# The second half's first layer norm from a turned input, with its scales and offsets spread over the partitions through DRAM

## The chip, the cores and the metric

The kernel runs on one core of one Trainium2 chip. The metric is the device time of one execution in microseconds, and it is taken as the median of several. Of the kernel before there are three runs: 2188.53, 2188.95 and 2190.12 us, median 2188.95.

## The reference

One transformer block on 2048 rows of 1024 numbers, in float32: layer norm, an attention with a memory that is carried from one segment of 512 rows to the next, and an MLP of width 3584.

```python
def _layernorm(x, axis=-1, eps=1e-5):
    m = jnp.mean(x, axis=axis, keepdims=True)
    v = jnp.var(x, axis=axis, keepdims=True)
    return (x - m) / jnp.sqrt(v + eps)

def _A_ref(x, wq, wk, wv, wo, beta):       # H = 32 heads of 32, N = 4 segments of L = 512
    q, k, v = ...                          # x @ wq, x @ wk, x @ wv, each as B, H, N, L, 32
    for s in range(N):
        logits = einsum("bhqd,bhkd->bhqk", q[s], k[s]) * scale + mask
        a_dot = einsum("bhqk,bhkd->bhqd", softmax(logits), v[s])
        a_mem = (phi(q[s]) @ M) / (phi(q[s]) @ z + 1e-6)
        outs.append(g * a_mem + (1.0 - g) * a_dot)
        M, z = M + phi(k[s]).T @ v[s], z + phi(k[s]).sum(0)
    return outs @ wo

h = x + _A_ref(_layernorm(x), wq, wk, wv, wo, beta)
y = _layernorm(h)
out = h + gelu(y @ w1 + b1) @ w2 + b2
```

The change concerns the very first line of this for rows 1024 to 2047: `_layernorm(x)` of the second half.

## The kernel before, in words

**Halves and slices.** The 2048 rows are done in two halves of 1024, one after the other in one loop; a half has two slices (`sl`) of 512 rows, which are the segments of the attention. A half runs through these stages: layer norm 1 and attention, the product with `wo`, layer norm 2, the first MLP product ("mixer"), and in half 1 the second MLP product for both halves.

**Number format.** TensorE multiplies in a rounded format, `fp32r`. So each operand is kept as two tiles, an upper part (rounded) and a lower part (the rest), and each product is three matmuls: upper by upper, lower by upper, upper by lower. The name of a tile ends in `h` or `l` accordingly: `wh`/`wl` for weights, `yh`/`yl` for the normalised input, `zh`/`zl` for the second layer norm's. The products of q, k and v are on lines 127 to 129 (tiles `qps`, `kps`, `vps` take the results in PSUM).

**Layer norm 1.** The products want `y` turned: features on partitions, 512 rows along the free axis, as `yh`, `yl` of 128 x 8 x 512. `ln1` (L214) loads four tiles `xt` of 128 rows x 1024 features; for each, VectorE takes the statistics (L134, L138), GpSimd makes the scale r = (v + eps)^-0.5 (L141, L142) and the offset -m r (L147), and ScalarE normalises the tile in place (L182), where scale and offset are one number a partition. Then `ln_transpose` (L156) turns it: per tile two groups of four transposes of 128 x 128 on TensorE (L161) into a PSUM tile `pt`, a copy by ScalarE into `yh` (L163) and a subtraction by VectorE into `yl` (L165). A layer norm of 512 rows so has 32 transposes in 8 groups. The bank of a group is taken in turn from tags "av", "pt", "pt"; the mixer's `dps` uses tag "pt" too.

**The mixer.** The first MLP product has 28 blocks of 128 features of w1, taken as 14 pairs (block j and block j + 14) in a form of the Strassen kind: instead of eight products of half size, seven, on sums of blocks. `pair(j)` (L1139) is 20 steps of PE, in five runs of four: S1 into `dps`, S3 into `bps`, `sixth(j+1)` (S2 of the next pair, into that pair's `bps`), A22 into `bps`, S4 into `dps`. Around them:

- `fetch` loads the raw weights `r0`, `r1` (named r1 and r2 in the code) of the pair after next, and its part `p1r` of the seventh product (L1113, L1115).
- `combine` (L1117) makes their sums s1 to s4 on GpSimd (L1121 to L1124).
- `made` (L1127) splits one sum into upper and lower: a ScalarE copy (L1136) and a VectorE subtraction (L1137), into tiles `sa` (even pairs) or `sb` (odd pairs).
- `u3` (L1164) is a VectorE read of the bank `bps` after S3; the A22 product then goes on adding to that bank. `ht` (L1033) are evictions of finished sums by VectorE, followed by gelu on ScalarE.

**The end of the first half (L1500 to L1513).** Pairs 0 to 4 of the mixer run alone. Pairs 5 to 13 are interleaved with the layer norm of the second half's first slice and the first three steps of its second slice: after every PE step of the mixer 0.17 of a step of the layer norm is issued. What is left of the second slice (`acts["ahead"]`) goes on during the second half's attention, 0.55 of a step per step there (L710, L758).

```python
acts["ahead"] = ln1(1, 1, gap=2)
interleave(chain(*(mixer.pair(j) for j in range(HP - 9, HP))),
           chain(ln1(1, 0, 2), islice(acts["ahead"], 3)), 0.17)
```

**What sets the order.** Within a half `in_order()` (L107) ties every instruction of an engine to the one written before it, so each engine works in the order in which the code is written and waits in that order: an instruction that waits holds up all behind it on its engine. At the change from half 0 to half 1 this order is opened and closed again, and the instructions that stand there, outside any such block, are placed by a scheduler. Loads are issued on the queue of SyncE (SP), in order as well.

**The start of the second half.** `attention_pool` (L338) makes the tile `mask` (a memset and a select, L341, L342) and the small tile `pat` (a memset and two selects, L355 to L357) on GpSimd, and loads the memory state. `load_block` (L330) loads and splits the first weights of k and q (L103, L104: ScalarE's copy, GpSimd's subtraction `wl`). Attention then runs as 16 units of 24 steps, each a group of four heads on one slice (ORDER); in a unit come the products of k and q, then their turned and regrouped copies: `side` (L443) holds a lower part on its way by DMA into `ks` and `qs`, and `pqk` (L563) is the first product of the scores. The two buffers `ks0` and `ks1` are first filled from `pat` by a VectorE cast (L676), in the first units only. The weights of v are split in four pieces by GpSimd (L693, tiles `wl`), and `pk` (L385) is a VectorE operation on the keys.

## Time and profile before

| | us |
|---|---|
| median of three runs | 2188.95 |
| the profiled execution | 2189.65 |
| its span in the trace | 2187.9 |
| of it: first half up to mixer pair 4 | 711.76 |
| mixer pairs 5 to 13 of the first half, with layer norm 1 of the next slice | 124.69 |
| first 44.55 us of the second half, with layer norm 1 of the last slice | 44.55 |
| the rest of the second half | 1306.9 |

The view of windows gives for the same stretches the busy time of each engine (in brackets the number of instructions), the granted TensorE clock, the share of time in which the DMA engines were busy, and their rate.

```profile
0.00:711.76 711.76, 694.60 (x3778) 558.64 (x3778) 443.48 (x1067) 430.16 (x1045) 318.81 (x531) 1.00 0.52 150
711.76:836.45 124.69, 123.81 (x561) 102.18 (x560) 72.17 (x108) 52.98 (x81) 48.12 (x45) 1.00 0.56 164
836.45:881.00 44.55, 43.67 (x222) 35.02 (x220) 33.71 (x79) 26.92 (x60) 24.42 (x42) 1.00 0.59 159
881.00:2187.90 1306.90, 1297.04 (x6379) 1054.87 (x6379) 813.65 (x1443) 590.78 (x1248) 558.56 (x589) 1.00 0.59 185
```

The engines stand in the order PE, weight loads, DVE (VectorE), ACT (ScalarE), POOL (GpSimd). A row of the trace that is quoted further down begins, in the timeline, with the start of the instruction and its duration, both in us, then engine, line, operation, destination <- sources and shapes, and in brackets the idle time of the engine before it with what ended it. In the lists by line, three numbers with strokes are the shortest, middle and longest duration in ns.

### The profile page before, as it was taken

Reading aid. Unit: us, or ns where it says so; the run is one execution under the profiler, and the core shown is the slowest. Engines: PE = TensorE matmul, PEld = TensorE weight load, DVE = VectorE, ACT = ScalarE, POOL = GpSimd, SP = SyncE. Lnnn points to the kernel's source line nnn. Section 1 sums busy time; section 2 is a strip of 40 time slices with the busy share of each in tenths; the row PEclk is TensorE's granted clock in tenths of the full one; section 3 lists DMA queues with packets and bytes.
Section 4 is the critical chain, followed back from the end, with each engine's and each line's share of the span. In section 5 each row is a group of like instructions: output and inputs, shape, how many; then the busy total and the mean of one; then the engine's idle time right before and its main releaser. Section 6 shows DMA issues by size and latency. Waiting matters only on the chain.

```text
span 2187.9 us, 33209 instructions
## 1 busy us (share of the span) xinstructions
PE 2159.1 (99%) x10937; PEld 1750.7 (80%) x10937; DVE 1363.0 (62%) x2696; ACT 1100.8 (50%) x2433; POOL 949.9 (43%) x1206
## 2 busy tenths in 40 slices
PE   7999999999999999999999999999999999999999
PEld 6777777778888887877777768888887888888887
DVE  6766666665745656766667655745666765577653
ACT  5777777762543445777777652643443232323221
POOL 5533335562444434433335561534445544256330
PEclk9999999999999999999999999999999999999999
DMA  6544445664575655544444664575569775576762
GB/s 181 136 107 106 106 106 136 192 199 164 156 209 155 183 163 138 139 108 108 107 108 131 197 192 147 173 217 161 171 189 378 270 231 187 190 245 229 247 223 92
DMA packets 352405, 376.20 MB, mean 172 GB/s; under 512 B 27214, under 2 KB 244330, under 8 KB 352234
## 3 DMA queue, kind: packets, MB, share of 16 engines
q1 hardware_dynamic: 288778, 336.98, 50.8%
q10 hardware_dynamic: 63456, 37.10, 5.6%
q8 instruction: 87, 1.43, 0.3%
q14 instruction: 84, 0.69, 0.1%
HBM read 241.27 MB, written 82.38 MB: 148 GB/s over the span
## 4 chain that ended last, share of the span: by engine, by line
PE 89%; DMA 4%; DVE 3%; ACT 1%; POOL 1%; issue 1%; SPq 0%; ACTq 0%; DVEq 0%; POOLq 0%
PE po L1405 22%; PE bps L1009 10%; PE cps L1009 7%; PE dps L1009 6%; PE pst L613 3%; PE po L627 3%; PE pqk L563 3%; PE kps L127 3%; PE pwo L127 3%; PE kps L128 3%; PE qps L127 2%; PE kps L129 2%; PE pwo L129 2%; PE pwo L128 2%; PE qps L128 2%; PE qps L129 2%
## 5 line engine op out<-in xcount | busy, mean ns | idle before, releaser
L565 DVE CUSTOM_DVE_ANT_0 pqk<-pqk,mask 128x512 f32<-128x512 f32 (+2 forms) x384 | 216.9, 565 | 241.3 <-PE pqk L563 214.8
L567 ACT ACTIVATE junk<-pqk,mx 128x512 f32<-128x512 f32 (+2 forms) x384 | 225.1, 586 | 137.1 <-DVE mx L565 130.5
L620 POOL TENSOR_SCALAR_AFFINE_SELECT e<-e 128x128 f32<-128x128 f32 (+1 forms) x384 | 136.2, 356 | 268.3 <-ACT e L616 254.5
L693 POOL TENSOR_TENSOR wl<-wr,wh 128x256 fp32r<-128x256 f32 x268 | 198.5, 756 | 112.1 <-PE pqk L563 88.1
L616 ACT ACTIVATE e<-pst 128x384 f32<-128x384 f32 (+1 forms) x384 | 200.3, 528 | 72.3 <-PE pst L613 70.3
L1415 DVE TENSOR_TENSOR c<-c,po 128x512 f32<-128x512 f32 x160 | 105.4, 683 | 152.4 <-PE po L1405 149.6
L563 PE MATMUL pqk<-ks,qs 96*128 96x512 f32 (+2 forms) x384 | 138.8, 362 | 7.1 <-DMA qs<-qq 4.3
L613 PE MATMUL pst<-qs,ks 104*128 104x512 f32 (+3 forms) x512 | 140.9, 318 | 1.0 <-ACT e L616 0.4
L613 PEld LDWEIGHTS pst<-qs,ks 104*128 104x128 f32 x512 | 95.7, 188 | 34.7 <-ACT e L616 10.7
L1405 PE MATMUL po<-w2h,zh 128*128 128x512 f32 x378 | 121.0, 390 | 0.7 <-DVE zh L1345 0.4
L1262 POOL TENSOR_TENSOR w2r<-w2r 128x512 f32<-128x512 f32 x54 | 85.9, 1603 | 73.7 <-DMA w2r<-in_B_w 50.0
L127 PE MATMUL qps<-yh,wh 128*128 128x512 f32 x256 | 113.8, 444 | 0.0
L127 PE MATMUL kps<-yh,wh 128*128 128x512 f32 (+1 forms) x264 | 113.0, 428 | 0.0
L1009 PE MATMUL bps<-zh,sb 128*128 128x512 f32 x336 | 111.1, 391 | 0.0
L1009 PE MATMUL bps<-zh,sa 128*128 128x512 f32 x336 | 110.8, 390 | 0.0
L1121 POOL TENSOR_TENSOR s<-r 128x512 f32<-128x512 f32 x28 | 44.1, 1575 | 143.4 <-DVE sa L1137 84.9
L127 PE MATMUL vps<-yh,wh 128*128 128x512 f32 x256 | 105.0, 410 | 0.0
L1405 PE MATMUL po<-w2h,hl 128*128 128x512 f32 x322 | 103.1, 390 | 0.4 <-DVE hl L1345 0.3
L128 PE MATMUL kps<-yl,wh 128*128 128x512 f32 (+1 forms) x264 | 102.4, 388 | 0.9 <-DVE yl L289 0.5
L129 PE MATMUL kps<-yh,wl 128*128 128x512 f32 (+1 forms) x264 | 101.8, 386 | 0.0
L128 PE MATMUL qps<-yl,wh 128*128 128x512 f32 x256 | 101.4, 396 | 0.0
L129 PE MATMUL qps<-yh,wl 128*128 128x512 f32 x256 | 101.0, 394 | 0.0
(271 smaller groups left out, 6211.1 us busy)
## 6 DMA issues: line engine op xcount, KB each, us to landing
hr<-h_dram SPq DMA_DIRECT2D x112, 448.0 KB, 5.4
w2r<-in_B_w SPq DMA_DIRECT2D x122, 256.0 KB, 4.4
r<-in_B_w SPq DMA_DIRECT2D x56, 512.0 KB, 4.7
ks<-kk SPq DMA_DIRECT2D x360, 64.0 KB, 2.0
qs<-qq SPq DMA_DIRECT2D x360, 64.0 KB, 2.0
h_dram<-ht ACTq DMA_DIRECT2D x84, 256.0 KB, 3.7
wx<-in_B_w SPq DMA_DIRECT2D x56, 256.0 KB, 3.5
o_dram<-side SPq DMA_DIRECT2D x52, 256.0 KB, 3.9
```

The lines of the kernel that those rows point to most:

```text
L127: nc.tensor.matmul(ps, ah, bh, start=first, stop=False)
L128: nc.tensor.matmul(ps, ah, bl, start=False, stop=False)
L129: acts["mm"] = nc.tensor.matmul(ps, al, bh, start=False, stop=last)
L563: nc.tensor.matmul(ps, u["qs"][0:96, j, i * P:(i + 1) * P], u["ks"][0:96, j, 0:n], start=True, stop=True)
L565: nc.vector.tensor_tensor_reduce(out=ps, in0=ps, in1=mask[:, 512 - n:512], op0=ALU.add, op1=ALU.min, scale=-SCALE, scalar=3.0e38, accum_out=m)
L567: at(now[0] + 1, lambda: nc.scalar.activation(acts["junk"][:, :n], ps, AF.Exp, bias=m, scale=-1.0, accum_out=u["mx"][:, 1, i, j:j + 1]))
L613: nc.tensor.matmul(ps[:, o:o + 512 - P * jk], u["ks"][:, j, jk * P:(jk + 1) * P], u["qs"][:, j, jk * P:512], start=True, stop=True)
L616: nc.scalar.activation(e, ps[:, :w], AF.Exp, scale=SCALE)
L620: nc.gpsimd.affine_select(d, d, pattern=[[0, 2], [1, P]] if n == 2 else [[1, P]], compare_op=ALU.is_ge, fill=0.0, base=0, channel_multipli ...
L693: nc.gpsimd.tensor_tensor(l[:, c], wr[:, c], raw(h)[:, c], op=ALU.subtract)
L1009: nc.tensor.matmul(ps, x_[:, c, :], y_[:, c, :], start=first and c == 0 and n == 0, stop=last and c == 3 and n == 2, skip_group_check=True)
L1405: nc.tensor.matmul(ps, x_[:, k], y_[k], start=opens and k == 0 and i == 0, stop=closes and k == self.KP - 1 and i == 2, skip_group_check=True)
```

## The change

The host passes the input a second time, turned (`A_xT`, 1024 x 2048). For the second half, layer norm 1 is done in two parts, one slice after the other:

- `row_scales` loads the four row tiles as before and takes the statistics as before. Scale and offset of the 4 x 128 rows go into one tile `rn` (128 x 8), and that is stored to DRAM as 8 x 128, one element at a time.
- `column_pairs` loads four tiles `xc` of the turned input (each 2 x 128 features x 512 rows), and `rows`: the 1024 numbers from DRAM, the same in every partition. VectorE multiplies a tile by the scales, GpSimd adds the offsets, ScalarE copies it into `yh` and VectorE subtracts into `yl`.

No transposes are left in it, and ScalarE no longer normalises there. The first slice's two parts and the second slice's `row_scales` stand beside mixer pairs 5 to 13, with 0.23 of a step per step in place of 0.17; the rest of the second slice's `column_pairs` goes beside attention as before. The first half is not touched.

```diff
+    def row_scales(half, sl):
+
+        rn = acts["rnp"].tile([P, 8], F32, name="rn", bufs=2)
+        xs = []
+        for t in range(4):
...
+            nc.sync.dma_start(xt, x[0, r0:r0 + P, :])
+            xs.append(xt)
+        for _ in range(3):
+            yield
+        for t in range(4):
...
+                nc.vector.bn_stats(st[:, i, :], xs[t][:, 512 * i:512 * i + 512])
...
+            nc.vector.bn_aggr(mv, st)
+            v = lnp.tile([P, 2], F32, name="v", bufs=3)
+            r = rn[:, t:t + 1]
+            nc.gpsimd.tensor_scalar(v[:, 0:1], mv[:, 1:2], 1.0, EPS, op0=ALU.mult, op1=ALU.add)
+            nc.gpsimd.tensor_tensor(r, v[:, 0:1], mhalf, op=ALU.pow)
+            nc.gpsimd.tensor_scalar(rn[:, 4 + t:5 + t], mv[:, 0:1], -1.0, r, op0=ALU.mult, op1=ALU.mult)
+            yield
+        nc.sync.dma_start(rn_dram[half, sl].rearrange("k p -> p k"), rn)
+        yield
+
+    def column_pairs(half, sl):
+
+        t0 = half * HT + 512 * sl
+        ws = []
+        for c in range(4):
+            w = lnp.tile([P, 2, 512], F32, tag="ln", name="xc", bufs=4)
+            nc.sync.dma_start(w, xt_[256 * c:256 * c + 256, t0:t0 + 512].rearrange("(c p) n -> p c n", p=P))
+            ws.append(w)
+            if c % 2:
+                yield
+        rows = acts["rnp"].tile([P, 2, 512], F32, name="rows", bufs=1)
+        nc.sync.dma_start(rows.rearrange("p a n -> p (a n)"),
+                          rn_dram[half, sl].rearrange("k p -> (k p)").partition_broadcast(P))
+        for _ in range(2):
+            yield
+        r, nb = (rows[:, i, :].unsqueeze(1).to_broadcast([P, 2, 512]) for i in range(2))
+        home = []
+        for c in range(5):
+            if c < 4:
+                nc.vector.tensor_tensor(ws[c], ws[c], r, op=ALU.mult)
+                nc.gpsimd.tensor_tensor(ws[c], ws[c], nb, op=ALU.add)
+                yield
+            if c > 0:
+                if not home:
+                    acts["y", half, sl] = acts["y", sl] = seg_tiles(sl, "y")
+                yh, yl = acts["y", sl]
+                k = slice(2 * c - 2, 2 * c)
+                home.append(nc.scalar.copy(yh[:, k, :], ws[c - 1]))
+                yield
+                nc.vector.tensor_tensor(yl[:, k, :], ws[c - 1], raw(yh[:, k, :]), op=ALU.subtract)
+                yield
...
-            acts["ahead"] = ln1(1, 1, gap=2)
+            acts["rnp"] = tc.alloc_tile_pool(name="rn1", bufs=1, reuse_waits="tile")
+            acts["ahead"] = column_pairs(1, 1)
             interleave(chain(*(mixer.pair(j) for j in range(HP - 9, HP))),
-                       chain(ln1(1, 0, 2), islice(acts["ahead"], 3)), 0.17)
+                       chain(row_scales(1, 0), column_pairs(1, 0), row_scales(1, 1), islice(acts["ahead"], 3)), 0.23)
```

What this does to the engines' order is seen at two places. In the changed kernel the lines after 231 are numbered some 60 higher (L165 is gone, L1137 is L1196, L1164 is L1223); the new ones are L278 (multiply), L279 (add), L286 (copy into `yh`) and L288 (subtraction into `yl`).

**The mixer's pair 9.** The work of GpSimd from the last `combine` operation for pair 9 to those for pair 10 (r0, r1: raw weights; s1 to s4: their sums), before:

```order
L1124 TENSOR_TENSOR s4_8031<-r0_7931,s2_8029 128x512
L141 TENSOR_SCALAR v_8089<-mv_8087 128x1
L142 TENSOR_TENSOR v_8089<-v_8089,mhalf_74 128x1
L147 TENSOR_SCALAR nb_8092<-mv_8087,v_8089 128x1
L1121 TENSOR_TENSOR s1_8146<-r1_8054 128x512
L1122 TENSOR_TENSOR s2_8147<-s1_8146,r0_8053 128x512
L1123 TENSOR_TENSOR s3_8148<-r0_8053,r1_8054 128x512
L1124 TENSOR_TENSOR s4_8149<-r0_8053,s2_8147 128x512
```

and now:

```order
L1183 TENSOR_TENSOR s4_8047<-r0_7956,s2_8045 128x512
L279 TENSOR_TENSOR xc_7948<-xc_7948,rows_8000 128x1024
L279 TENSOR_TENSOR xc_7950<-xc_7950,rows_8000 128x1024
L279 TENSOR_TENSOR xc_7981<-xc_7981,rows_8000 128x1024
L1180 TENSOR_TENSOR s1_8160<-r1_8071 128x512
L1181 TENSOR_TENSOR s2_8161<-s1_8160,r0_8070 128x512
L1182 TENSOR_TENSOR s3_8162<-r0_8070,r1_8071 128x512
L1183 TENSOR_TENSOR s4_8163<-r0_8070,s2_8161 128x512
L279 TENSOR_TENSOR xc_7983<-xc_7983,rows_8000 128x1024
```

Three adds of 128 x 1024 stand between the two groups of four, and the fourth behind them, where three operations on 128 x 1 stood. VectorE at the same place, from the evictions `ht` of pair 8 to `u3` of pair 9, before:

```order
L1033 TENSOR_TENSOR ht_8142<-bps_7985,p1r_7817 128x512
L1033 TENSOR_TENSOR ht_8172<-dps_8065,u2_7998 128x512
L1137 TENSOR_TENSOR sa_8182<-s2_8147,sa_8182 128x512
L1137 TENSOR_TENSOR sa_8185<-s1_8146,sa_8185 128x512
L165 TENSOR_TENSOR yl0_7951<-pt_8157,yh0_7950 128x4x128
L1137 TENSOR_TENSOR sa_8202<-s3_8148,sa_8202 128x512
L1164 TENSOR_TENSOR u3_8217<-bps_8108,p1r_7935 128x512
```

and now:

```order
L278 TENSOR_TENSOR xc_7981<-xc_7981,rows_8000 128x1024
L1092 TENSOR_TENSOR ht_8156<-bps_8007,p1r_7822 128x512
L1092 TENSOR_TENSOR ht_8181<-dps_8082,u2_8020 128x512
L1196 TENSOR_TENSOR sa_8191<-s2_8161,sa_8191 128x512
L1196 TENSOR_TENSOR sa_8194<-s1_8160,sa_8194 128x512
L288 TENSOR_TENSOR yl0_8107<-xc_7950,yh0_8106 128x1024
L1196 TENSOR_TENSOR sa_8211<-s3_8162,sa_8211 128x512
L278 TENSOR_TENSOR xc_7983<-xc_7983,rows_8000 128x1024
L1223 TENSOR_TENSOR u3_8228<-bps_8120,p1r_7960 128x512
```

The subtraction into `yl` is twice as large and reads `xc` in SBUF where it read `pt` in PSUM, and a multiply has come in ahead of the evictions and another ahead of `u3`.

**The start of the second half.** GpSimd from the lower parts of the first k and q weights on (`wl` of 128x1024; then `wl` of 128x256 are the v weights), before:

```order
L104 TENSOR_TENSOR wl_8747<-wr_8744,wh_8746 128x1024
L104 TENSOR_TENSOR wl_8753<-wr_8750,wh_8752 128x1024
L141 TENSOR_SCALAR v_8770<-mv_8768 128x1
L142 TENSOR_TENSOR v_8770<-v_8770,mhalf_74 128x1
L147 TENSOR_SCALAR nb_8773<-mv_8768,v_8770 128x1
L341 MEMSET mask_8724 128x512
L355 MEMSET pat_8737 8x4
L342 AFFINE_SELECT mask_8724<-mask_8724 128x128
L356 AFFINE_SELECT pat_8737<-pat_8737 8x4
L693 TENSOR_TENSOR wl_8792<-wr_8763,wh_8791 128x256
L357 AFFINE_SELECT pat_8737<-pat_8737 8x4
L693 TENSOR_TENSOR wl_8792<-wr_8763,wh_8791 128x256 x3
```

and now:

```order
L105 TENSOR_TENSOR wl_8753<-wr_8750,wh_8752 128x1024
L105 TENSOR_TENSOR wl_8759<-wr_8756,wh_8758 128x1024
L279 TENSOR_TENSOR xc_8575<-xc_8575,rows_8627 128x1024
L279 TENSOR_TENSOR xc_8577<-xc_8577,rows_8627 128x1024
L752 TENSOR_TENSOR wl_8791<-wr_8769,wh_8790 128x256 x4
L400 MEMSET mask_8730 128x512
L414 MEMSET pat_8743 8x4
L401 AFFINE_SELECT mask_8730<-mask_8730 128x128
L415 AFFINE_SELECT pat_8743<-pat_8743 8x4
L416 AFFINE_SELECT pat_8743<-pat_8743 8x4
L279 TENSOR_TENSOR xc_8594<-xc_8594,rows_8627 128x1024
```

Two adds and all four pieces of the v weights now stand ahead of `mask` and `pat`. VectorE there, from `side` of the first keys to `side` of the first queries, before:

```order
L443 TENSOR_TENSOR side_8732<-kps_8756,side_8732 128x512
L676 CAST ks0_8733<-pat_8737 8x2048
L165 TENSOR_TENSOR yl1_8801<-pt_8802,yh1_8800 128x4x128
L385 SCALAR_TENSOR_TENSOR pk_8847,zc_8846<-e_8821,r_8828 128x512
L165 TENSOR_TENSOR yl1_8801<-pt_8831,yh1_8800 128x4x128
L676 CAST ks1_8734<-pat_8737 8x2048
L134 BN_STATS st_8859<-xt_8630 128x6 x2
L138 BN_AGGR mv_8862<-st_8859 128x2
L443 TENSOR_TENSOR side_8732<-qps_8808,side_8732 128x512
```

and now:

```order
L502 TENSOR_TENSOR side_8738<-kps_8762,side_8738 128x512
L735 CAST ks0_8739<-pat_8743 8x2048
L288 TENSOR_TENSOR yl1_8800<-xc_8575,yh1_8799 128x1024
L278 TENSOR_TENSOR xc_8594<-xc_8594,rows_8627 128x1024
L444 SCALAR_TENSOR_TENSOR pk_8837,zc_8836<-e_8815,r_8822 128x512
L735 CAST ks1_8740<-pat_8743 8x2048
L288 TENSOR_TENSOR yl1_8800<-xc_8577,yh1_8799 128x1024
L502 TENSOR_TENSOR side_8738<-qps_8802,side_8738 128x512
```

Between the two `side` operations stand two subtractions of 128 x 1024 and a multiply where there were two subtractions of half that size and a set of statistics.

More of the change, by code (lines that the diff above doesn't have):

```diff
@@ L49, in raw, with build @@
     return ap.bitcast(F32)
-def build(tc, x, wq, wk, wv, wo, beta, w1, b1, w2, b2, out):
+def build(tc, x, xt_, wq, wk, wv, wo, beta, w1, b1, w2, b2, out):
     nc = tc.nc
@@ L90, in build @@
     t_dram = {n: [dram.tile([P, 512], F32, name=f"t{n}_dram{k}") for k in range(FB // 2)] for n in "36"}
+    rn_dram = {k: dram.tile([8, P], F32, name=f"rn_dram{k[0]}{k[1]}") for k in ((1, 0), (1, 1))}
     mz_dram = dram.tile([P, NG * 132 + 96], F32, name="mz_dram")
@@ L230, in ln1 @@
                             fold=lambda src, t4: ln_transpose(src, *home(), t4, ("av", "pt", "pt"), slow=True))
+    def row_scales(half, sl):
+        rn = acts["rnp"].tile([P, 8], F32, name="rn", bufs=2)
+        xs = []
+        for t in range(4):
+            xt = lnp.tile([P, D], F32, tag="ln", name="xt", bufs=4)
+            r0 = half * HT + (4 * sl + t) * P
+            nc.sync.dma_start(xt, x[0, r0:r0 + P, :])
[3 more added lines that the diff above has]
+        for t in range(4):
+            st = lnp.tile([P, 2, 6], F32, name="st", bufs=3)
+            for i in range(2):
+                nc.vector.bn_stats(st[:, i, :], xs[t][:, 512 * i:512 * i + 512])
+            mv = lnp.tile([P, 2], F32, name="mv", bufs=3)
+            nc.vector.bn_aggr(mv, st)
[7 more added lines that the diff above has]
+        yield
@@ L1450, in build @@
         ab.release()
+        if "rnp" in acts:
+            acts.pop("rnp").release()
         zx = acts["zx"] = tc.alloc_tile_pool(name=f"zx{half}", bufs=1, side="right", reuse_waits="tile")
@@ L1547, in build @@
     top.close()
-_INS = ["A_x", "A_wq", "A_wk", "A_wv", "A_wo", "A_beta", "B_w1", "B_b1", "B_w2", "B_b2"]
+_INS = ["A_x", "A_xT", "A_wq", "A_wk", "A_wv", "A_wo", "A_beta", "B_w1", "B_b1", "B_w2", "B_b2"]
 def kernel(**inputs):
@@ L1559 @@
     arrays, args = {}, []
+    inputs = {**inputs, "A_xT": np.asarray(inputs["A_x"])[0].T}
     for name in _INS:
```

## The prediction

> **What bounds the kernel now.** I read the page first: the busy shares, then the chain of work that ended last.
>
> ```profile
> span 2187.9 us, 33209 instructions
> PE 2159.1 (99%) x10937; PEld 1750.7 (80%) x10937; DVE 1363.0 (62%) x2696; ACT 1100.8 (50%) x2433; POOL 949.9 (43%) x1206
> PE 89%; DMA 4%; DVE 3%; ACT 1%; POOL 1%; issue 1%; SPq 0%; ACTq 0%; DVEq 0%; POOLq 0%
> ```
>
> TensorE is busy 99% of the span and carries 89% of the chain. So work taken from PE is gained, and every new wait of PE is lost; work on DVE, ACT or POOL costs only where PE comes to wait for it. The profiled execution took 2189.65 us, 1.75 more than its span, and lies 0.7 above the median of 2188.95. I make the sum as a difference and apply it to the median.
>
> The change sits in the stretch from mixer pair 5 of the first half to the second attention unit of the second. The timeline of PE shows its frame:
>
> ```profile
> 711.76 0.39 PE L1009 MATMUL dps<-zh,sb 128*128 128x512 f32 x1
> 717.20 0.39 PE L1009 MATMUL bps<-zh,sa 128*128 128x512 f32 x1
> 719.92 0.39 PE L1009 MATMUL bps<-zh,sb 128*128 128x512 f32 x1
> 725.36 0.39 PE L1009 MATMUL dps<-zh,sa 128*128 128x512 f32 x1
> 836.45 0.39 PE L127 MATMUL kps<-yh,wh 128*128 128x512 f32 x1
> ```
>
> Pair 5 starts at 711.76 and pair 6 at 725.36: a pair is 13.60 us. Inside it `sixth` of the next pair starts at +5.44 (717.20) and needs that pair's S2 split; the A22 product starts at +8.16 (719.92) and adds to a bank that DVE must first have read into u3. These are the two due times for DVE. The first kps of the second half, "A" below, is at 836.45.
>
> **What goes.** The timeline and the list for tile pt:
>
> ```profile
> L161 PE MATMUL pt<-ident,xt x64: 270/272/274, 740.3 to 878.5; 128*128 128x128 f32 x64
> 811.40 0.47 PE L1009 MATMUL dps<-zh,sa 128*128 128x512 f32 x1 [0.88 <-DVE ht L1033]
> 816.70 0.39 PE L1009 MATMUL bps<-zh,sa 128*128 128x512 f32 x1
> 816.93 0.60 PE L161 MATMUL pt<-ident,xt 128*128 128x128 f32 x4
> 817.28 0.48 PE L1009 MATMUL bps<-zh,sb 128*128 128x512 f32 x1
> 817.60 0.39 PE L1009 MATMUL bps<-zl,sb 128*128 128x512 f32 x1
> ```
>
> 64 transposes are 16 groups of four. Products start 0.227 apart; without the group, the one at 817.60 would have started at 817.16, so a group costs PE 0.44 us. The wait at 811.40 is for a bank of tag pt, which the transposes turn by one extra step; it goes too. Checked from the frame: nine pairs without transposes, the last one product shorter, take 8 x 13.60 + 10.88 = 119.7 us and would put A at 831.4; it is at 836.45. **The mixer gains 5.0 us** (eight groups, the wait and small rests), **attention 8 x 0.44 = 3.5**. If nothing came to wait, that is 8.5 us.
>
> **What comes.** Eight DVE multiplies, eight POOL adds and eight ACT copies of 128x1024, eight DVE subtractions of 128x1024 that now read SBUF where sixteen of 128x512 read PSUM; eight ACT normalisations go. Durations, and how the two engines meet:
>
> ```profile
> L921 DVE TENSOR_TENSOR hb<-ht,b2c x16: 1170/1208/1227, 510.9 to 1379.7; 128x1024 f32<-128x1024 f32 x16
> L104 POOL TENSOR_TENSOR wl<-wr,wh x2: 2398/2403/2408, 832.6 to 835.4; 128x1024 fp32r<-128x1024 f32 x2
> L103 ACT CAST wh<-wr 128x1024 fp32r<-128x1024 f32 x1 | 1.0, 1037 | 0.0
> 1678.74 2.62 POOL L1318 TENSOR_TENSOR hr<-hr 128x896 f32<-128x896 f32 x1 [2.54 <-DMA hr<-h_dram]
> 1679.29 3.01 DVE L1345 TENSOR_TENSOR zl<-hr,zl 128x896 fp32r<-128x896 f32 x1
> 1681.33 2.13 POOL L1262 TENSOR_TENSOR w2r<-w2r 128x512 f32<-128x512 f32 x1
> 1684.05 1.08 DVE L1345 TENSOR_TENSOR hl<-hr,hl 128x896 fp32r<-128x896 f32 x1
> ```
>
> DVE 1.2 (1.15 in a run), POOL 2.4, ACT 1.04. The last four rows matter most: the DVE operation takes 1.08 alone, but 3.01 when it starts beside a POOL operation. It ends 1.0 after POOL's end at 1681.36, and POOL's next one, 2.13 instead of the 1.29 of its kind, waits in turn until DVE is done. So DVE operations with two SBUF inputs and POOL operations take turns whole, and the one that waits goes next.
>
> [...]
>
> **The mixer.** DVE's frame in an undisturbed pair:
>
> ```profile
> 713.85 1.66 ACT L1136 CAST sa<-s 128x512 fp32r<-128x512 f32 x3 [0.44 <-ACT ht L1026]
> 714.50 2.99 DVE L1137 TENSOR_TENSOR sa<-s,sa 128x512 fp32r<-128x512 f32 x3 [1.85 <-ACT sa L1136]
> 715.32 1.61 POOL L1121 TENSOR_TENSOR s<-r 128x512 f32<-128x512 f32 x1 [5.48 <-DVE sa L1137]
> 717.41 0.68 DVE L1164 TENSOR_TENSOR u<-bps,p1r 128x512 f32<-128x512 f32 x1
> 718.60 1.29 POOL L1123 TENSOR_TENSOR s<-r,r 128x512 f32<-128x512 f32 x1
> 723.44 1.28 DVE L134 BATCH_NORM_STATS2 st<-xt 128x6 f32<-128x512 f32 x2
> 724.76 0.21 DVE L138 BATCH_NORM_AGGREGATE mv<-st 128x2 f32<-128x12 f32 x1
> ```
>
> S2 is split at +2.7 (714.50) and u3 read at +5.65 (717.41) to +6.3: 2 us of slack each. A POOL combine operation takes 1.25 to 1.3. POOL's order now puts three adds ahead of the four combine operations of pair 10 (shown with the change). Step by step, in offsets of the pair:
> - Pair 8: DVE's second multiply at +3.8, its S3 split to +5.55, POOL's add +5.55 to +7.9. DVE's subtraction, due at +6.9, takes its turn at +7.9; the rest follows a microsecond late, the third multiply ends at +11.95, its add runs to +14.4, which is +0.8 of pair 9.
> - Pair 9: the combine operations start only there: s2 at +3.3, ACT's copy +3.9, DVE's S2 split after s3, to +5.15 (due +5.44). s4 takes +5.15 to +6.4, then S1 7.0, subtraction 8.1, S3 8.7, multiply 9.85, u3 10.5. Due at +8.16: **PE waits 2.3**.
> - Pair 10: DVE alternates with three combine operations and subtracts before its two evictions, so ACT's copy of S2 ends at +5.85, the split at +6.5 (**1.0 late**), and with two more combine operations between S3 and the last subtraction u3 ends at 12.0 against 9.2 (**2.8**).
>
> Sum 6.1; taking turns less strictly, one waiting operation fewer in each pair, 3; with no turns 0.5. I take 6.1 because the rows above show the turns. In pairs 6 and 11 two rows of statistics (1.45 us each) stand ahead of u3: 2.7 + 3 x 0.6 + 2 x 1.45 = 7.4, read to +8.05, just in time.
>
> **The start of the second half.**
>
> ```profile
> 835.42 2.40 POOL L104 TENSOR_TENSOR wl<-wr,wh 128x1024 fp32r<-128x1024 f32 x1 [0.37 <-ACT wh L103]
> 840.05 0.53 POOL L341 MEMSET mask<- 128x512 f32 x1
> 840.63 0.10 POOL L355 MEMSET pat<- 8x4 f32 x1
> 841.17 0.19 POOL L356 TENSOR_SCALAR_AFFINE_SELECT pat<-pat 8x4 f32<-8x4 f32 x1
> 843.55 2.13 POOL L693 TENSOR_TENSOR wl<-wr,wh 128x256 fp32r<-128x256 f32 x3
> 844.98 1.78 DVE L676 CAST ks<-pat 8x2048 fp32r<-8x2048 f32 x1
> 848.71 1.22 DVE L676 CAST ks<-pat 8x2048 fp32r<-8x2048 f32 x1
> 851.40 0.64 DVE L443 TENSOR_TENSOR side<-qps,side 128x512 fp32r<-128x512 f32 x1
> 854.31 0.47 PE L563 MATMUL pqk<-ks,qs 96*128 96x512 f32 x1 [0.16 <-DMA qs<-side]
> ```
>
> Before, POOL made mask and pat early; the first pqk (A+17.9) followed DVE's lower half of q (ends 852.04) by 2.27 of DMA, with PE waiting 0.16. Now two adds and the four v splits stand ahead of mask and pat: wl of q ends A+1.0 (it began at 835.42 because ACT normalised a row first; now 0.35 earlier), the adds end 5.8, the v splits 8.7, and mask and pat take 1.6 (840.05 to 841.36, and one more select of 0.2): pat is ready at 10.3. DVE's ks cast, at +8.5 before, waits for pat to 10.4. Behind it queue: cast 11.6, subtraction 12.75, multiply 13.9, pk 14.5, POOL's add to 16.85, second cast 18.05, subtraction 19.2, and the lower half of q 19.8. The first pqk can start at A+22.05; PE, with three groups fewer (17.7 - 1.3), is there at 16.4: **5.65 us**. Then the fourth add (21.15 to 23.5) holds back DVE's next weight cast and POOL's split of the k weights, which PE wants at 23.4 and gets at 26.1: **2.7**. The third pqk waits 0.6 for its bank. Sum 8.95, less 0.5 for small waits of the old start that go: 8.5. Without turns q is 2.3 earlier (3.3 to wait), the weights wait 0.75, the bank 0.3: 4.4.
>
> **Sum.** -5.0 - 3.5 + 6.1 + 8.5 = +6.1 us: 2195.8 from the profiled execution, 2195.0 from the median.
>
> **Scales through DRAM.** The trace has no store of 1024 single elements. Bounds:
>
> ```profile
> q1 hardware_dynamic: 288778, 336.98, 50.8%
> q10 hardware_dynamic: 63456, 37.10, 5.6%
> b2c<-in_B_b SPq DMA_DIRECT2D x2, 512.0 KB, 8.8
> ```
>
> Share times 16 times span, by packets: 62 ns on q1, 31 on q10. 64 packets on each of 16 engines are 2 to 4 us behind some 2 of start. The scales of the first block are ready some 11 us into pair 6 (736.6), the store has landed by 741 to 743, and the broadcast load, like b2c in shape, takes at most 8.8: 750 to 752. DVE's first multiply comes up at 750.5. I count nothing: q's short packets are nearest, and DVE has over a microsecond to spare there. The extra transposed loads (512 KB each, two pairs ahead) collide with nothing that is due.
>
> **Rivals.**
> - *Scales late.* If the store takes 12 us, rows land near 755 and DVE's first multiply ends 756.5, or +3.9 of pair 8. Being in order, it holds the eviction behind it, S2 and the second multiply: u3 of pair 8 comes near +9.5, 1.3 late, and pair 9's chain starts 1 to 2 later still. Some 3 us more, 2198; it decides from 8 us of store on. [...]
> - *No turns.* DVE and POOL share without blocking: -8.5 + 0.5 + 4.4 - 0.5 = -4.1, 2184.8. Against it: the 3.01 row.
> - *All hidden.* Only PE's savings count: -8.5, 2180.5. For it: DVE 62%, POOL 43% busy. Against it: the 2 us slacks, and pat behind two adds.
>
> **How the numbers follow.** Forecast 0.50 (own range 2191 to 2198.5; about a fifth of it within 0.2%, which is 4.4 us and about what a measurement of this kernel can tell from no change); scales late 0.13; no turns or weak ones 0.25 (2184.5 to 2191, nearly all within 0.2%); all hidden 0.12. So slower 0.40 + 0.13 = 0.53, within 0.2% 0.10 + 0.22 = 0.32, faster 0.03 + 0.12 = 0.15. The range leaves a tenth at each end: 2183 to 2199.5. Break-even lies at 8.5 us of new waiting, slower by over 0.2% at 12.9; 14.6 are counted.
>
> **What would show it.** In pair 9 and 10, PE waiting for DVE u3 (or S2) at a bps product, 2 to 3 us each; at the second half's start the ks cast released by POOL's pat near A+10, the first pqk waiting about 6 us for DMA qs, and then kps for POOL's wl. DVE multiplies of 1.2 us where POOL is idle and 2 to 3.5 beside an add. If those pqk and u3 waits are under a microsecond, I am wrong and the time falls; if DVE's first multiply idles for the DMA of rows, the scales are late.

## The result, and the profile after

| | before | changed |
|---|---|---|
| median, us (4 runs each) | 2189.53 | 2220.62 |
| profiled execution, us | 2189.65 | 2220.98 |
| its span, us | 2187.9 | 2219.3 |

The ratio is 1.014 (95% interval 1.0126 to 1.0155): 31 us slower, where 6.1 slower was forecast and 2199.5 was the end of the range. One execution below, the fourth of e1, took 3047.1 us at a granted clock of 0.655; it is left out. The page of the changed kernel, busy shares:

```profile
PE 2164.3 (98%) x10873; PEld 1752.7 (79%) x10873; DVE 1366.3 (62%) x2696; ACT 1092.1 (49%) x2417; POOL 978.4 (44%) x1214
```

The 64 transposes are gone (10937 matmuls, now 10873), yet PE's busy time rose by 5 us. The shares do not tell why; the view of windows by stage does. Pair 5 starts at 711.95 now, and the first kps ("A") stands at 862.71 (first two rows: changed kernel, third: the kernel before, whose first stage is in the table ahead of the change):

```profile
711.95:862.71 150.76, 129.34 (x530) 104.37 (x528) 85.61 (x119) 46.92 (x72) 63.45 (x58) 0.91 0.65 176
862.71:2219.30 1356.59, 1339.47 (x6569) 1088.80 (x6567) 839.22 (x1510) 614.48 (x1300) 594.16 (x626) 1.00 0.59 183
836.45:2187.90 1351.45, 1340.71 (x6601) 1089.89 (x6599) 847.36 (x1521) 617.69 (x1307) 582.98 (x631) 1.00 0.59 184
```

The mixer's nine pairs went from 124.69 to 150.76, **+26.1 where the forecast had +1.1** (-5.0 and +6.1). From A to the end it is 1351.45 to 1356.59, **+5.1 where the forecast had +5.0** (-3.5 and +8.5). So nearly all of the miss lies in the mixer. Its waits are in the timeline of PE (the last number is the idle time ahead, and what ended it):

```profile
768.82 0.79 PE L1068 MATMUL bps<-zh,sb 128*128 128x512 f32 x1 [10.41 <-ACT sb L1195]
790.25 0.50 PE L1068 MATMUL bps<-zh,sb 128*128 128x512 f32 x1 [2.23 <-DVE u L1223]
807.64 0.50 PE L1068 MATMUL bps<-zh,sa 128*128 128x512 f32 x1 [1.87 <-DVE u L1223]
854.89 0.76 PE L1068 MATMUL bps<-zh,sb 128*128 128x512 f32 x1 [6.76 <-ACT ht L1085]
884.29 0.76 PE L622 MATMUL pqk<-ks,qs 96*128 96x512 f32 x1 [5.33 <-DMA qs<-side]
```

The middle two are the forecast's pairs 9 and 10, and the last its start of the second half. The first and the fourth, 17.2 us, were not in it. Nor was what follows each long wait; windows behind five of these waits, with the granted clock as the third number from the end:

```profile
768.82:774.44 5.62, 5.62 (x13) 4.41 (x14) 5.58 (x7) 2.74 (x5) 2.77 (x1) 0.51 0.24 67
790.25:794.70 4.45, 4.45 (x13) 3.50 (x14) 2.25 (x3) 2.81 (x4) 4.37 (x4) 0.63 0.22 63
807.64:811.60 3.96, 3.96 (x11) 3.18 (x12) 2.56 (x4) 1.86 (x3) 0.48 (x2) 0.61 0.85 250
854.89:859.60 4.71, 4.71 (x11) 3.74 (x12) 1.25 (x2) 0.73 (x2) 2.37 (x1) 0.50 0.40 111
884.29:893.90 9.61, 8.85 (x23) 6.78 (x24) 8.20 (x12) 3.52 (x8) 7.31 (x7) 0.50 0.66 174
```

In these five windows PE runs at a mean clock of 0.50 to 0.63. Busy time times what the clock lacks is what that costs, an estimate from these rows: 2.75, 1.65, 1.54, 2.36 and 4.4, so 8.3 us in the mixer and 4.4 behind the first pqk. That accounts for the mixer: the clean 119.7, waits of 21.4 (with a small one of 0.15) and 8.3 of half clock are 149.4 of the 150.8.

**The wait of 10.4 us**, read backwards. SyncE's queue (start, and duration of the issue), then landing times by issue (the last number), then GpSimd, VectorE and ScalarE:

```profile
737.67 0.37 SPq L256 DMA_DIRECT2D rn_dram<-rn  x1
738.13 1.05 SPq L265 DMA_DIRECT2D xc<-in_A_xT  x2
739.27 10.55 SPq L1172 DMA_DIRECT2D r<-in_B_w  x2
756.79 0.69 SPq L270 DMA_DIRECT2D rows<-rn_dram  x1
...
rn_dram<-rn SPq DMA_DIRECT2D x1, 4.0 KB, 9.9
r<-in_B_w SPq DMA_DIRECT2D x2, 512.0 KB, 19.5
...
760.21 1.26 POOL L1180 TENSOR_TENSOR s<-r 128x512 f32<-128x512 f32 x1 [17.44 <-DMA r<-in_B_w]
765.13 1.23 DVE L278 TENSOR_TENSOR xc<-xc,rows 128x1024 f32<-128x1024 f32 x1 [7.56 <-DMA rows<-rn_dram]
766.27 0.68 DVE L1092 TENSOR_TENSOR ht<-dps,u 128x512 f32<-128x512 f32 x1
766.99 0.72 ACT L1085 ACTIVATE ht<-ht,b1c 128x512 f32<-128x512 f32 x1 [8.66 <-DVE ht L1092]
768.15 1.66 ACT L1195 CAST sb<-s 128x512 fp32r<-128x512 f32 x3 [0.44 <-ACT ht L1085]
```

Two things are late. The raw weights of pair 9, whose second load was issued at 735.04 before, now stand on the queue behind a store that waits for the scales until 737.67, and behind two turned loads; they land after 18.8 and 20.3 us, and GpSimd begins their sums at 760.21 in place of 742.52. And the scales land at 765: VectorE's multiply waits for them, the eviction `ht` queues behind the multiply, ScalarE's S2 copy behind the gelu of that eviction. The S2 sum itself was ready by 762.8, 5.3 us ahead of its copy at 768.15. So of the two it is the scales that set the length of this wait; late raw weights alone would have made some 5 us of it (an estimate from these rows: PE was due at 758.4, and it starts 0.7 after the copy does).

**The wait of 6.8 us** is the second slice's store. Timeline of SyncE's queue and of VectorE:

```profile
829.61 0.37 SPq L256 DMA_DIRECT2D rn_dram<-rn  x1
842.20 0.34 SPq L270 DMA_DIRECT2D rows<-rn_dram  x1
851.18 2.36 DVE L278 TENSOR_TENSOR xc<-xc,rows 128x1024 f32<-128x1024 f32 x2 [5.92 <-DMA rows<-rn_dram]
853.46 0.69 DVE L1092 TENSOR_TENSOR ht<-dps,u 128x512 f32<-128x512 f32 x1
```

By the list of issues the store takes 12.5 us, the load 9.0. The scheduler has put the second slice's first two multiplies ahead of three of the mixer's last evictions on VectorE, so PE waits for rows that only attention needs.

### The profile page after: what moved, and what is told of

The parts are those of the page before. It is cut to its first block, busy times and chain, and to the rows that moved or that the text cites. A ratio compares the mean times of both kernels' runs of the same rounds, so it can differ in the third digit from the quotient of the medians.

```text
span 2219.3 us, 33103 instructions
## 1 busy us (share of the span) xinstructions
PE 2164.3 (98%) x10873; PEld 1752.7 (79%) x10873; DVE 1366.3 (62%) x2696; ACT 1092.1 (49%) x2417; POOL 978.4 (44%) x1214
## 4 chain that ended last, share of the span: by engine, by line
PE 88%; DMA 4%; DVE 3%; ACT 2%; POOL 2%; issue 1%; SPq 0%; ACTq 0%; POOLq 0%; DVEq 0%
PE po L1464 23%; PE bps L1068 8%; PE cps L1068 7%; PE dps L1068 5%; PE pst L672 3%; PE po L686 3%; PE pqk L622 3%; PE kps L128 3%; PE kps L130 3%; PE kps L129 3%; PE qps L128 3%; PE qps L129 2%; PE pwo L128 2%; PE qps L130 2%; PE vps L128 2%; PE pwo L130 2%
## 5 line engine op out<-in xcount | busy, mean ns | idle before, releaser
L1068 PE MATMUL bps<-zh,sb 128*128 128x512 f32 x336 | 115.4, 405 | 19.4 <-ACT sb L1195 10.4
```

Source lines behind the costliest of these rows:

```text
L1068: nc.tensor.matmul(ps, x_[:, c, :], y_[:, c, :], start=first and c == 0 and n == 0, stop=last and c == 3 and n == 2, skip_group_check=True)
```

## The experiments

Theory A: the store of single elements holds back what is queued behind it. Its rivals: the turned loads crowd the queues (B), or SyncE's wait for the scales is what delays the loads (C). For the waits that were forecast, the theory is that GpSimd's adds and the turns of the two engines make u3 and the first pqk late.

**e1_store_whole.**

```diff
-        nc.sync.dma_start(rn_dram[half, sl].rearrange("k p -> p k"), rn)
+        nc.sync.dma_start(rn_dram[half, sl].rearrange("k p -> (k p)").rearrange("(p k) -> p k", k=8), rn)
...
+        rk = rows.rearrange("p a n -> p (a n)").rearrange("p (n k) -> p k n", k=8)
+        r, nb = (rk[:, 4 * i:4 * i + 4, :].unsqueeze(1).to_broadcast([P, 2, 4, P]) for i in range(2))
```

> The scales are stored as they lie, 8 numbers of a partition side by side (128 pieces of 32 B in place of 1024 of 4 B), and multiply and add read the rows with a step of 8 numbers; all orders of the engines stay. Theory A (the store of single elements holds the DMA queues for some 10 us, and the raw weights behind it land late): the waits of PE of 10.4 us (at 768.8) and 6.8 us (at 854.9) go, with the half clock after them (2.7 and 2.1 us), so some 22 us less than 2220.6: 2197 to 2202. What stays are waits for u3 (2.2 and 1.9) and for the first pqk (5.3). Theory B (the four turned loads crowd the queues): within 2 us of 2220.6. Theory C (SyncE's queue waits for the scales to be made before it issues the next loads): within 2 us of 2220.6, since the store still waits for the scales.

Measured 2210.8 (median of three; ratio to before 1.010, 1.0077 to 1.0124); the profiled execution, 2205.04, is the shortest of them. The store now lands after 1.4 us:

```profile
rn_dram<-rn SPq DMA_DIRECT2D x1, 4.0 KB, 1.4
```

Both long waits are gone: PE waits 1.5 us for S2 in pair 8, 2.6 in pair 9, nothing at the mixer's end, and the mixer's stage is 135.1 in place of 150.8. The rest of the expectation missed: reading with a step made a multiply 2.1 us and an add 2.9 to 3.4, and the turned loads still stand ahead of the raw weights. GpSimd's first sum of pair 9 starts at 749.04, released by their landing.

**e2_rows_for_columns.**

```diff
-            nc.sync.dma_start(w, xt_[256 * c:256 * c + 256, t0:t0 + 512].rearrange("(c p) n -> p c n", p=P))
+            nc.sync.dma_start(w, x[0, t0 + P * c:t0 + P * c + P, :].rearrange("p (c n) -> p c n", c=2))
```

> The four loads of the turned input are replaced by loads of as many bytes from the rows of the input, 4 KB in a piece, so the second half's layer norm works on unturned numbers; the rest stays. Theory A (element store): within 3 us of 2220.6, the wait of 10 us stays. Theory B (the turned loads, with their pieces of 2 KB, crowd the queues): 8 to 20 us less.

Measured 2214.4 (two runs), 6.2 less: outside both. The wait of 10.4 is 9.15, so it is not the form of the turned loads that makes it.

**e3_multiply_behind.**

```diff
-                nc.vector.tensor_tensor(ws[c], ws[c], r, op=ALU.mult)
+                op = nc.vector.tensor_tensor(ws[c], ws[c], r, op=ALU.mult)
+                if "last" in acts:
+                    behind(op)
```

> The first two multiplies of the second slice are held behind the mixer's last VectorE operation, in place of ahead of its last three evictions; nothing else moves. If the wait of 6.8 us at 854.9 is that place (evictions queued behind a multiply whose rows land late), it goes with its 2.1 us of half clock, and the start of attention pays some of it back, since pat and the lower half of q still come late: 4 to 9 us less than 2220.6, 2212 to 2217. Rival: the wait is only moved to the first pqk, and the time stays within 2 us.

Measured 2217.0 (2214.0 to 2218.8), the upper end of what was expected; the profiled execution, 2214.01, is the shortest of them. The wait of 6.8 is gone, and the mixer's stage is 140.7, 10.1 shorter. From A to the end it is 1360.6, 4.0 longer: attention paid part of it back.

**e4_before_with_store.**

```diff
+                if self.half == 0 and j == 9:
+                    nc.sync.dma_start(rn_dram.rearrange("k p -> p k"), ident[:, 0:8])
```

> The kernel before with nothing added but one store of 128 x 8 numbers, 4 B a piece, ahead of the raw weights of pair 9 on SyncE's queue (its numbers are used by nothing). Theory A: the raw weights of pair 9 land some 10 us later, PE waits 7 to 11 us for the S2 split in pair 8 and runs at half clock for some 5 us after, 10 to 14 us more than before: 2199 to 2204. Theories B and C: within 1.5 us of 2189.5.

A miss: 2188.05 against 2187.84 (0.9991 to 1.0013). The store had nothing to wait for and was issued at 724.2, where what stands behind it is not needed for long. It landed after 13.5 us, by the list of issues.

**e5_store_in_place.**

```diff
+                if self.half == 0 and j == 9:
+                    nc.sync.dma_start(rn_dram.rearrange("k p -> p k"), self.src[8]["S1"][:, 0, 0:8])
```

> As the store added to the kernel before, but it now waits for the first weight sum of pair 8, made at about 739, so that it stands on SyncE's queue right ahead of the raw weights of pair 9 (issued at 740.8 before). Theory A (a store of 1024 single elements holds back what is queued behind it for 10 to 13 us; the first try cost nothing because 13 us of slack lay there): the raw weights land at 753 to 756 in place of 745, the S2 split of pair 9 comes 1 to 5 us late, with one or two spells of half clock: 2190 to 2198, and the landing of these raw weights is 12 us or more. Theory B (the store delays only itself): landing under 7 us, time within 1.5 us of 2189.

The expectation named the wrong row: the loads at 740.8 are pair 10's, those of pair 9 were issued at 723.99 and 735.04. Measured 2190.1 (1.0007, 0.9994 to 1.0019), by the time alone no difference. The landings decide it (issues of 737.5 to 738.6; then ScalarE's stores issued from 738 to 765, in this kernel and in the kernel before):

```profile
r<-in_B_w SPq DMA_DIRECT2D x2, 512.0 KB, 14.7
rn_dram<-s SPq DMA_DIRECT2D x1, 4.0 KB, 9.4
...
h_dram<-ht ACTq DMA_DIRECT2D x4, 256.0 KB, 9.3
...
h_dram<-ht ACTq DMA_DIRECT2D x4, 256.0 KB, 2.8
```

The raw weights take 14.7 us for 4.2, and stores from the other queue are held too. GpSimd's first sum of pair 9 comes at 754.98; PE waits only 1.53, since slack was there. So there are four kernels for one date, that of this sum: before 742.5, turned loads with a store of whole pieces 749.0 (+6.5), element store without turned loads 755.0 (+12.5), both 760.2 (+17.7). In all but the first SyncE's queue also waits until 737.4 to 737.7 (C); what the element store does by itself is the landing, 14.7 for 4.2. **Theory A holds, and B and C account for the smaller part; no run separates those two.** A sum that comes 12.5 us late costs PE 1.53 us here; in the changed kernel the rows of scales, late through the same store, come on top, and they end the wait.

**e6_pe_rows_no_add** and **e7_pe_rows** take DRAM out of the path. Of e7 (e6 drops the add too; both hold the multiplies as e3 does):

```diff
-        nc.sync.dma_start(rn_dram[half, sl].rearrange("k p -> p k"), rn)
+        for i in range(2):
+            pr = psum.tile([P, 512], F32, tag="qk", name="pr", bufs=2)
+            for t in range(4):
+                nc.tensor.transpose(pr[:, t * P:(t + 1) * P], rn[:, 4 * i + t:4 * i + t + 1].to_broadcast([P, P]), ident)
+            nc.scalar.copy(rows[:, i, :], pr)
```

> Scales and offsets are spread over the partitions by TensorE (eight transposes of a column repeated 128 times into two banks a slice, two ScalarE copies) in place of the store and the load, the first two multiplies of the second slice are held behind the mixer's last VectorE operation, and GpSimd's eight adds are left out, so the offsets are not applied. Turns theory (GpSimd's adds ahead of the weight sums and of pat make u3, S2 and the first pqk late): the waits for u3 go to under 0.5 us, that for the first pqk to under 2.5, the clock stays whole nearly everywhere: 2182 to 2190. Rival (the loads and VectorE's own work make them late): within 4 us of the same kernel with the adds.

> As the one before, with the adds: the orders of VectorE and GpSimd are those of the kernel with the multiplies held behind. Without store and row loads the waits of 9 to 10 us and 6.8 us and the half clock after them are gone, four groups of transposes cost 1.8 us; what stays are u3 (two of 2 to 2.5 us), the first pqk (5 to 6.5), the k weights (0.8 to 2) and some 5 to 9 us of half clock: 2200 to 2208.

**e12_pe_rows_no_mul_no_add** drops the multiplies as well.

> As e6_pe_rows_no_add, with VectorE's eight multiplies left out too, so the second half's first layer norm applies neither scale nor offset; loads, statistics, copies and subtractions stay. If multiplies and adds, with their turns, are the whole of what the removal of the transposes pays back, only the 8.5 us saved and the 1.8 us of the four new groups are left: 2181 to 2186, under the kernel before. Rival (the loads of both forms of the input, or the subtractions that now read SBUF, cost as much): 2188 and more, with waits of PE for u3 or S2 of over 1 us.

e7: 2203.2 (1.006, 1.004 to 1.0081), as expected. e6: 2193.2 (1.0017, 1.0006 to 1.0029), outside both of its ranges. e12: 2189.8 (1.0017, 1.0004 to 1.003), what its rival expected, with a wait for u3 of over 1 us. PE's waits for u3 in pairs 9 and 10 and for the first pqk, in e7, e6 and e12:

```profile
778.85 0.79 PE L1073 MATMUL bps<-zh,sb 128*128 128x512 f32 x1 [2.27 <-DVE u L1228]
796.23 0.50 PE L1073 MATMUL bps<-zh,sa 128*128 128x512 f32 x1 [1.97 <-DVE u L1228]
865.03 0.76 PE L627 MATMUL pqk<-ks,qs 96*128 96x512 f32 x1 [5.86 <-DMA qs<-side]
...
780.39 0.50 PE L1072 MATMUL bps<-zh,sb 128*128 128x512 f32 x1 [2.68 <-DVE u L1227]
795.88 0.50 PE L1072 MATMUL bps<-zh,sa 128*128 128x512 f32 x1 [1.57 <-DVE u L1227]
860.50 0.47 PE L626 MATMUL pqk<-ks,qs 96*128 96x512 f32 x1 [3.23 <-DMA qs<-side]
...
774.59 0.50 PE L1069 MATMUL bps<-zh,sb 128*128 128x512 f32 x1 [0.30 <-DVE u L1224]
790.08 0.50 PE L1069 MATMUL bps<-zh,sa 128*128 128x512 f32 x1 [1.57 <-DVE u L1224]
852.88 0.47 PE L623 MATMUL pqk<-ks,qs 96*128 96x512 f32 x1 [1.42 <-DMA qs<-side]
```

**The adds are not what makes u3 late.** Without them both waits stay; without the multiplies pair 9's goes, and pair 10's stays at 1.57. What stands right ahead of that u3 is the subtraction from SBUF, 2.31 us with its turn; that it makes the wait is read from the rows, as no run leaves it out. By stage, from pair 5 to A: 129.7, 128.8, 125.8 (before 124.7); from A to the end: 1356.8, 1352.7, 1350.6 (before 1351.5). So in these profiles the adds cost 0.9 in the mixer and 4.1 in attention, the multiplies 3.0 and 2.1. The medians say 10 us for the adds (the profiled e6 is the longest of its ten), and they don't tell e12 from e6. Even with neither the mixer gains nothing in the profile: the four new groups, waits of 1 us of TensorE for GpSimd's `rn`, and 1.9 for u3 use up most of what the transposes cost; 1.4 us of it has no row.

**e8_pe_rows_pat_first.**

```diff
+                if "last" in acts:
+                    tc.add_manual_dep(op.ins, acts["patop"].ins.name, NOSYNC, reason="program order")
```

> As e7_pe_rows, with mask and pat made ahead of the second slice's first two adds on GpSimd. If pat behind the adds is what makes the first pqk late, its wait falls by 2 to 4 us and with it one or two spells of half clock (1.7 us each): 3 to 7 us less than e7_pe_rows. Rival (VectorE's chain of cast, subtraction and multiply ahead of the lower half of q is as long anyway): within 1.5 us of it.

2199.5 (1.0032 to 1.0066), by the medians 3.6 under e7, as the theory expected; but e7's interval is 1.004 to 1.0081, so the times don't tell them apart. In the traces VectorE's first ks cast no longer waits for pat (2.80 us in e7), but the wait ahead of the first pqk is 5.81, and that product starts at A + 22.1 in place of 23.7. GpSimd's v weights (four in 5.79 us, 2.85 in e7) moved in beside VectorE's chain, and both stretched (the first ks cast 1.56 us, the subtraction 1.66, the multiply 1.75; in e7 1.22 to 1.23 each): of the 2.8 us, 1.6 are left. PE waits as long as before, since it comes to this product 1.6 us earlier too. That pat comes late is a part of the delay, not its whole.

**e9_placed** and **e10_placed_late.**

```diff
+            for n, _ in enumerate(chain(*(mixer.pair(j) for j in range(HP - 9, HP)))):
+                if n % 20 in (8, 11, 14, 16, 18):
+                    next(side, None)
...
-                    acc += 0.55 if half else 0.7
+                    acc += (0.55 if b + c >= 18 else 0) if half else 0.7
```

> As e7_pe_rows, but the side work of the mixer's pairs 5 to 13 is issued after steps 8, 11, 14, 16 and 18 of a pair, that is behind the read of u3, in place of 0.23 of a step after every step. If u3 is late because VectorE has a subtraction and a multiply queued between the splits and u3 (the waits of 2.3 and 2.0 us were there without the adds too), both waits fall under 0.5 us and a spell or two of half clock goes: 4 to 7 us less than e7_pe_rows, 2193 to 2199. Rival (VectorE is short of time in those pairs, so that the wait only moves to the S2 split): within 2 us of e7_pe_rows.

> As e9_placed, and the second slice's multiplies, adds and subtractions start only after step 18 of attention, behind the lower half of the first queries. If they are what holds VectorE between the first keys and the first queries (four of them, 4.9 us with their turns, and pat behind two adds), the first pqk's wait of 5.9 us, the small waits beside it and 6.8 us of half clock go: 11 to 15 us less than e9_placed, 2180 to 2187, under the kernel before. Rival (the work is only moved to where VectorE has less time, and the second slice comes late for the third unit): less than 6 us gained, with a new wait of PE for yl.

Neither gains: 2206.0 (1.0061 to 1.009), 2.8 above e7 where the rival had at most 2, and 2208.1 (1.0077 to 1.0109), where the rival's new wait for yl is not seen. Timeline of PE, two rows of e9 and one of e10:

```profile
764.68 0.79 PE L1073 MATMUL bps<-zh,sa 128*128 128x512 f32 x1 [2.52 <-DVE u L1228]
779.28 0.50 PE L1073 MATMUL bps<-zh,sa 128*128 128x512 f32 x1 [1.93 <-ACT sa L1200]
...
902.50 0.77 PE L627 MATMUL pqk<-ks,qs 96*128 96x512 f32 x1 [5.45 <-DMA qs<-qq]
```

The waits went to other pairs, to the S2 split, and from the first unit's pqk (2.17 us in e10, 5.85 in e9) to a later one. In neither of these two places does the work cost less; that there is too much of it for the two engines together is our reading.

**e11_rows_in_psum.**

```diff
-                nc.gpsimd.tensor_tensor(ws[c], ws[c], nb, op=ALU.add)
+                (nc.gpsimd if sl else nc.vector).tensor_tensor(ws[c], ws[c], nb, op=ALU.add)
```

(and, for the first slice, `rows` is the list of the two PSUM banks).

> As e7_pe_rows, but for the first slice scales and offsets stay in the two PSUM banks, VectorE reads them there, and VectorE also makes the four adds that GpSimd made. Turns theory (only VectorE operations with all inputs in SBUF take turns with GpSimd): multiplies and adds of the first slice take 1.2 to 1.3 us each, also beside a GpSimd operation, where the same multiplies took up to 3 us; but VectorE has 4.8 us more to do, u3 of pairs 9 and 10 stays 2 to 4 us late, and the time stays within 4 us of e7_pe_rows. Rival (shared bandwidth, the place of the operand makes no difference): these operations too stretch to 2 us and more beside GpSimd, and the time rises by over 4 us.

2201.0 (1.0058, 1.0039 to 1.0078), within 4 us of e7; u3 of pair 9 comes 4.94 late, over the expected 4, that of pair 10 only 0.30. Timeline around pair 9, VectorE and GpSimd; the last two rows are from e6, the same pair of operations with the scales in SBUF:

```profile
777.44 1.21 DVE L285 TENSOR_TENSOR xc<-xc,pr 128x1024 f32<-128x1024 f32 x1
777.59 1.27 POOL L1191 TENSOR_TENSOR s<-r,r 128x512 f32<-128x512 f32 x1 [0.63 <-DVE sa L1205]
...
778.52 1.21 DVE L281 TENSOR_TENSOR xc<-xc,rows 128x1024 f32<-128x1024 f32 x1
778.67 2.19 POOL L1186 TENSOR_TENSOR s<-r,r 128x512 f32<-128x512 f32 x1 [0.62 <-DVE sa L1200]
```

The multiply's own duration tells nothing here: from SBUF it takes 1.21 to 1.23 too, in the changed kernel and in e7. Near the 3 us that were expected here it came in e9, where two of the eight took 2.30 and 3.11. GpSimd's sum, which starts 0.15 us after the multiply, tells: beside a multiply with two SBUF inputs it stretches to 2.19, beside one with an input in PSUM it takes 1.27. That the turns are real is shown; the old subtraction, which read `pt` in PSUM, took none (all 24 took 0.68 to 0.69), and the new one does (1.21 to 2.53 in the changed kernel).

No version with the turned input came under the kernel before; the nearest, e6 and e12, leave out the adds or all of the arithmetic and are no layer norm.

## Why the prediction was wrong, point by point

- *What goes, 8.5 us.* Nothing speaks against it: in the mixer, the clean 119.7 with the waits and the half clock is within 1.4 of what was measured.
- *Scales through DRAM: "I count nothing".* **This step failed.** The store took 9.9 and 12.5 us where 4 to 6 were worked out from packets of other shapes; worse, it was priced for itself alone. What it holds back was left out: the raw weights behind it, also by its wait for the scales, and the load of rows, issued at 756.8 and not at 743, since the issues ahead of it on the queue took 10.55 and 5.42 us (why they took so long is not shown). Rows landed at 765, not at 750 to 752. The rival *scales late* had the mechanism (a multiply that holds eviction and S2), with a chance of 0.13. It had rows near 755 and a price of 3 us; with rows at 765 the wait is 10.4.
- *"The extra transposed loads collide with nothing that is due."* Failed: with a store that lands after 1.4 us, and the queue's wait for the scales, the first sum of the raw weights is still 6.5 us late (e1).
- *The second slice's multiplies.* Two of them stand ahead of three of the mixer's last evictions, and the prediction has no term for them. 6.8 us; e3 shows it.
- *The price of a wait.* Each was counted as its length. Half clock behind them cost 8.3 us in the mixer and 4.4 behind the first pqk: the term that was missing everywhere. Which waits bring it is in the last section.
- *Pairs 9 and 10, 2.3 and 3.8.* Measured 2.23 and 1.87. The first is so near by luck: the reason that was given, GpSimd's adds ahead of the weight sums, falls with e6. It is VectorE's own queue ahead of u3: in pair 9 the multiply (e12), in pair 10, by the rows, a subtraction that takes its turn. Of pair 10's 3.8, the 1.0 for S2 did not come.
- *The sign for turns, multiplies of 2 to 3.5 us.* It did not come: all eight took 1.21 to 1.23. The turns stand in the subtractions, up to 2.53, and in GpSimd's sums.
- *The start of the second half.* Right: first pqk 5.65 forecast, 5.33 measured; the lower half of q ended at A + 19.4 (19.8 forecast); k weights 0.75 (2.7), third pqk 0.45 (0.6). e6 confirms that the adds hold it, by about half. **That the stage came out at +5.1 against +5.0 is luck.** A later product of the same kind, in the changed kernel and before:

```profile
915.50 0.47 PE L622 MATMUL pqk<-ks,qs 96*128 96x512 f32 x1 [2.22 <-DMA qs<-qq]
881.57 0.47 PE L563 MATMUL pqk<-ks,qs 96*128 96x512 f32 x1 [0.62 <-DMA qs<-qq]
```

  Counted from A, 52.79 and 45.12: by here 7.7 us are lost and not 5.0. Waits that are 7.3 longer than before, 4.4 of half clock and the 3.5 that the transposes gave back make 8.2. From 310 to 460 us after A 2.3 us of it come back; 1.3 of that are waits which the kernel before has there (0.98 for qs at 1234.99) and the changed one not, or shorter. The forecast has nothing on that stretch.
- *No turns* is refuted by e11 and by the stretched rows, *all hidden* by the waits.

## What to carry to other kernels

The price of a small DMA lay here in what stood behind it on its queue, in what the queue itself waited for, and in its pieces, not in its bytes: the same 4 KB took 9.9 us to land in 1024 pieces and 1.4 in 128. Ask for each load behind it when it is due, and how much slack is left once the new loads are in. A step that moved from PSUM operands to SBUF operands on VectorE changed more than its duration: the subtraction, 0.68 to 0.69 us before, took 1.21 to 2.53 at twice the size, in turns with GpSimd. And in the versions of this kernel, bound by TensorE, a wait cost its length and, behind 29 of the 30 windows of 3.41 us at full clock that were idle for 1.85 us or more, at least one window at half clock besides; in e7, where the longest wait was 5.86 us, the waits and the half clock cost more than the work that was saved.

## What the runs showed of the hardware that was not expected

- A store of 1024 elements of 4 B took 9.4 us to land in e5, 9.9 and 12.5 in the changed kernel and 13.5 in e4, and for 10 us hardly anything else got through: from 739.2 to 749 the changed kernel's DMA moved 14 GB/s, the kernel before 135, and e1, with 128 pieces of 32 B, 303. ScalarE's stores, on another queue, were held as well (9.3 us in e5 for 2.8 in the kernel before).
- **The edges of the half clock lay on a fixed grid.** In windows of half a microsecond of the changed kernel (the mean clock of the window in which it changes places the edge) it falls at 760.72, 791.44, 808.51, 852.88 and 883.60 and rises at 774.38, 794.86, 811.92, 859.71 and 893.84: all of them whole multiples of 3.413 us apart, to 0.01. So, to some hundredths, are the edges within every other profile here that has any, each with a start of its own. Windows on this grid around pair 9's wait, in the changed kernel (2.23 us) and in e6 (2.68 us); the first columns are the stretch and PE's busy time in it, the clock is third from the end:

```profile
788.03:791.44 3.41, 1.19 (x5) 1.01 (x6) 3.38 (x5) 0.48 (x1) 1.77 (x1) 1.00 0.40 119
791.44:794.86 3.42, 3.42 (x10) 2.65 (x9) 1.22 (x2) 2.33 (x4) 3.34 (x4) 0.50 0.29 81
...
775.75:779.16 3.41, 1.96 (x9) 1.30 (x7) 3.41 (x3) 0.00 (x0) 2.71 (x3) 1.00 0.00 0
779.16:782.58 3.42, 2.19 (x10) 1.80 (x10) 2.46 (x4) 1.05 (x2) 1.70 (x1) 1.00 0.02 5
```

  The shorter wait lies in one window, which is idle for 2.22 of 3.41 us, and the next is at half clock; the longer one is split over two, 1.45 and 1.23 idle, and costs no clock. Over the eleven profiles that have edges, from 680 to 900 us, 30 windows at full clock were idle for 1.85 us or more, and 29 were followed by half clock; of 26 that were idle for 1.2 to 1.85 us, 2 were. So in these profiles about half a window idle decided, and the phase of the grid made the price of a wait of 1.9 to 3.7 us (once and twice the 1.85, an estimate from these counts) a matter of where it fell. At half clock less was enough to stay there: of 63 such windows the 31 that were idle for at most 0.40 us were all followed by full clock, the 32 that were idle for 0.51 or more all by another at half. So the short wait of 0.75 us for the k weights, behind the first pqk, cost a whole window more (890.43 to 893.84, at 0.50).
- An operation with one SBUF input stretched as well: the second cast of `pat` into ks took 3.27 us beside an add in e7 (3.29 in the changed kernel), and 1.22 in e6, where the adds are left out.
